# Normalising attention through a transposed, DRAM-spread row of reciprocals, and two early score blocks

## The chip, the cores and the metric

One NeuronCore of a Trainium2 chip runs the whole program. The metric is device time in microseconds of one execution; the kernel before takes 704.56 us as the median of three executions (704.35 to 704.77). TensorE is written PE, VectorE DVE, ScalarE ACT, GpSimd POOL, SyncE (here the main DMA queue) SP.

## The reference, cut to what matters

Attention with pooled queries, then two feed-forward blocks. Batch 2, 8 heads, 1152 keys, 576 pooled queries, head size 64, model width 512.

```python
q_pool = q.reshape(B, H, S // 2, 2, D).mean(axis=3)          # 576 queries
scores = (1.0 / np.sqrt(D)) * np.matmul(q_pool, k^T)
scores = scores - max(scores)
attn = exp(scores);  attn = attn / (sum(attn) + 1e-09)
out = attn @ v                                                # [B, H, 576, 64]
x = out as [1152 tokens, 512];  h = x @ w_in;  x = softplus(h) @ w_out      # d_ff 2048
xn = x / sqrt(mean(x*x) + 1e-06) * rms_g
y = (silu(xn @ w_gate) * (xn @ w_val)) @ w_out2               # d_ff 1536
```

The division by the row sum is what the change is about: every query row of every head has one sum, and the kernel divides after the product with v.

## The kernel before, in words

**Pairs.** The 16 (batch, head) matrices are worked off as eight pairs `pb` of two heads. The 576 queries of a head are four tiles of 128 (`x` = 0 to 3, NF = 4) and a rest of 64; the rests of the two heads share a fifth tile, `x` = NF, the shared tile.

**One tile.** `qk` (line 434) multiplies queries with keys: a query is split in a high and a low part, so that a tile of one head takes 6 matmuls of 384 columns into one of two score areas in PSUM: area A for head 0 and for the shared tile (there 12 matmuls), area B for head 1. `softmax` (457) reduces the negated maximum `nm` on DVE (463) and runs Exp on ACT (465), whose accumulator puts the row sum into a column of `den` (128 x 9: four tiles of each head and the shared one). An area is free again when its Exp has read it. `flip` (473) and `flip_m` (732, for the shared tile) transpose the probabilities on PE, four blocks of 128 x 128 to a PSUM bank, and ACT or DVE copies the bank to `pt`. `av` (492) multiplies `pt` with v into such a bank and copies it to `O`, which holds the output of the pair transposed: head size of both heads along the partitions, 576 queries along the columns.

**Two banks.** All transposes and `av` take their banks in turn from a ring of two (`tbank`, 470): what is to write a bank waits until everything that touched the use two before it is done.

**Normalising.** `scales` (509) adds 1e-9 to `den`, takes reciprocals, and copies each reciprocal 64 times beside itself into `rd` (five blocks of 128 x 128). `spread` (525) transposes those blocks on PE (four blocks in part 0, one in part 1), so that the reciprocals lie along the columns, in the same bank ring, and DVE multiplies `O` with them into `y` (540, 547); then `y` is split in a high and a low part for the next stage.

**Order.** The loop at lines 766 to 799 emits the work; PE's order is the order of emission. `turn` (724) gives the transposes of a tile as a list: T[0], T[1] (4 + 4 of head 0), T[2], T[3] (4 + 4 of head 1), T[4] (the ninth block of both heads); for the shared tile T[0], T[1], T[2] (4, 4, 1). In a tile `x` < 4 the order is T[0], (spread of the pair before, in tiles 1 and 2), scores of `x`+1 into A, T[1], `av` of the tile before, T[2], T[3], scores into B, T[4]. The scores B emitted in tile 3 are those of the next pair's tile 0; its scores A are emitted in the shared tile, after T[0] and T[1].

**The planner.** For the other engines the class `Plan` (63) makes a list schedule out of declared costs: each operation has one or two engines on which it may run, a due time follows from what comes after it, and operations start in order of time. Where ACT and DVE can both do one, SLACK (2.0 us) decides how readily ACT takes it; WAIT (5.0 us) says from which difference in due time an engine is kept for a more urgent operation. DMAs are planned on the SP queue in the same way.

**After attention.** Line 800 on: weights come as 64-bit numbers and are decoded (`decode`, 296) into a high and a low part on ACT, DVE and POOL, 68 pieces in all, 32 of them for the first feed-forward block; slots for 18 pieces open before attention is over, the rest when its buffers are free. Three blocks of 384 tokens go through 16 steps of the first block (a step is 24 matmuls, `terms`, 584) and then 12 of the second.

Of the kernel before, what the change touches and what calls it, by code (L numbers as in the profile page):

```python
# [12 lines left out]
F32 = mybir.dt.float32  # L13
# [3 lines left out]
ALU = mybir.AluOpType  # L17
# [3 lines left out]
P = 128  # L21
B, H, S, D = 2, 8, 1152, 64
SQ = S // 2
# [5 lines left out]
CK = S // P  # L29
NP = B * H // 2  # L30
NF = SQ // P
N = 384
NBLK = NT // N
KB = S // N
# [1 line left out]
MIDDLE = 8  # L36
AFTER = 2 * J1 + 24
SEM = 0.1
SLACK = 2.0
WAIT = 5.0  # L40
WARM = 16
MM = N / 2400 + 0.014

# [19 lines left out]
class Plan:  # L63
# [13 lines left out]
    def op(self, opts, fn, r=(), w=(), lat=0.0, after=()):  # L77
        o = Op()
        o.fn, o.opts, o.lat = fn, opts, lat
        o.deps, o.after, o.succ = set(), set(after), []  # L80
        o.n = len(self.ops)
        for keys, writes in ((r, False), (w, True)):
            for b, part in keys:
                o.deps |= self.before(b, part, writes)
        for keys, writes in ((r, False), (w, True)):
            for b, part in keys:
                (b.writers if writes else b.readers).setdefault(part, []).append(o)
                if not b.ops or b.ops[-1] is not o:
                    b.ops.append(o)
        o.deps.discard(o)  # L90
        self.ops.append(o)
        if opts[0][0] == "PE":
            self.pe.append(o)
        return o
# [101 lines left out]
def dve(n, fast=False, psum=False):  # L196
    t = 0.157 + n / (1920 if fast else 960)
    return ("DVE", t) if psum else ("DVE", t, 1)


def act(n, sbuf=True):
    return "ACT", n / 1400 + (0.28 if sbuf else 0.2)


def pool(n):
    return "POOL", 0.05 + n * 0.00275
# [3 lines left out]
def body(ctx: ExitStack, tc: tile.TileContext, kT, qT, v, w1, w1o, wg, wv, w2o, rg, outT):  # L210
    nc = tc.nc
# [3 lines left out]
    plan = Plan()  # L215
    op = plan.op

    const = ctx.enter_context(tc.tile_pool(name="const", bufs=1))
    ident = const.tile([P, P], F32, name="ident")
    make_identity(nc, ident)  # L220
    ones = const.tile([P, 1], F32, name="ones")
# [26 lines left out]
    def ring(which, tag, shape, dtype=F32, bufs=1):  # L248
        b = plan.ring(tag, bufs, sb(which, tag, shape, dtype, bufs))
        owned[which].append(b)  # L250
        return b

    def copy(e, out, in_):
        if e == "ACT":
            nc.scalar.copy(out, in_)  # L255
        else:
            engines[e].tensor_copy(out, in_)  # L257

    def tt(e, out, in0, in1, o):
        engines[e].tensor_tensor(out=out, in0=in0, in1=in1, op=o)  # L260
# [35 lines left out]
    def decode(n):  # L296
# [26 lines left out]
        if b in third:  # L323
# [4 lines left out]

    qx = [[[fixed("ea"[z], f"q{s}{'AB'[h]}{z}", [P, NF * P + P], F32R) for s in "hl"] for h in range(2)]
          for z in range(2)]  # L330
# [4 lines left out]
    for z in range(2):  # L335
        for h in range(2):
            for s in range(2):
                c = NF * P + (D if h == 0 else 0)
                op([dve(D)], lambda e, b=qx[z][h][s], c=c: copy(e, b()[:, c:c + D], zero), w=[(qx[z][h][s], "z")])

    st = [dict() for _ in range(NP)]

    def prep(pb):
# [7 lines left out]
        kcuts = [(c, slice(c * N, c * N + N), N) for c in range(KB)]  # L351
        f = NF * P
        qcuts = ((0, slice(0, P), P), (1, slice(P, SQ), SQ - P))
# [78 lines left out]
    units = {}  # L432

    def qk(pb, x, h):
# [4 lines left out]
        sc = units[pb, x, h]["s"]  # L439
        heads = (h,) if x < NF else (0, 1)  # L440
        todo = [(hh, z) for hh in heads for z in range(2)]
# [50 lines left out]
    def av(pb, x):  # L492
        s = st[pb]
        pt = units[pb, x, 0]["pt"]
        t = tbank()
        n = P if x < NF else D

        def go(e):
            for c in range(CK):
                for h in range(2):  # L500
                    rhs = pt()[:, c, h, :] if x < NF else pt()[:, c, 0, h * D:h * D + D]
                    nc.tensor.matmul(t()[h * D:h * D + D, :n], lhsT=s["v"][h]()[:, c, :], rhs=rhs,  # L502
                                     start=(c == 0), stop=(c == CK - 1))
        op([("PE", 0.1 + CK * 0.24 * n / P)], go, r=[(pt, None), (s["v"][0], None), (s["v"][1], None)],
           w=[(t, None)])
        o = s["O"]
        op([dve(n, psum=True), act(n, False)], lambda e: copy(e, o()[:, x * P:x * P + n], t()[:, :n]), r=[(t, None)], w=[(o, x)])

    def scales(pb):
        s = st[pb]  # L510
        den = s["den"]
        behind = [units[pb + 1, 0, h]["mx"] for h in range(2) if (pb + 1, 0, h) in units]
        rd = s["rd"] = ring("a", "rdb", [P, NF + 1, 2, D])
        o = op([("DVE", 0.17, 1)], lambda e: nc.vector.tensor_scalar(out=den(), in0=den(), scalar1=1e-9, scalar2=None,
                                                                    op0=ALU.add), w=[(den, None)])
        o.deps.update(behind)
        op([("DVE", 0.25, 1)], lambda e: nc.vector.reciprocal(den(), den()), w=[(den, None)])
        op([dve(NF * P), act(NF * P)], lambda e: copy(
            e, rd()[:, :NF], den()[:, :2 * NF].rearrange("p (h x) -> p x h", h=2).unsqueeze(3).to_broadcast([P, NF, 2, D])),
           r=[(den, None)], w=[(rd, 0)])  # L520
        op([dve(P), act(P)], lambda e: copy(
            e, rd()[:, NF], den()[:, 2 * NF:].unsqueeze(2).to_broadcast([P, 2, D])),
           r=[(den, None)], w=[(rd, 1)])

    def spread(pb, part):
        s = st[pb]
        rd, o = s["rd"], s["O"]
        bank = tbank()
        if part == 0:
            s["y"] = ring("a", "y", [P, SQ])  # L530
        y = s["y"]
        f = NF * P
        xs = range(NF) if part == 0 else (NF,)

        def go(e):
            for i, x in enumerate(xs):
                nc.tensor.transpose(bank()[:, i * P:(i + 1) * P], rd()[:, x].rearrange("p h d -> p (h d)"), ident)  # L537
        op([("PE", 0.09 * len(xs) + 0.03)], go, r=[(rd, part)], w=[(bank, None)])
        if part == 0:
            op([dve(f, psum=True)], lambda e: nc.vector.tensor_tensor(out=y()[:, :f], in0=o()[:, :f], in1=bank()[:, :f], op=ALU.mult),  # L540
               r=[(bank, None), (o, None)], w=[(y, 0)])
            return

        def rest(e):
            for h in range(2):
                p = slice(h * D, h * D + D)
                nc.vector.tensor_tensor(out=y()[p, f:], in0=o()[p, f:], in1=bank()[p, h * D:h * D + D], op=ALU.mult)
        op([("DVE", 0.46)], rest, r=[(bank, None), (o, None)], w=[(y, 1)])
        b, k = divmod(pb, H // 2)
        cuts = ((0, 0, N), (1, 0, SQ - N)) if b == 0 else ((1, SQ - N, N), (2, 0, N))  # L550
        q0 = 0
        for t, a, z in cuts:
            m = z - a
            i = slice(q0, q0 + m)
            o2 = slice(a, z)
            xh, xl = X[t]
            op([dve(m, True), act(m)], lambda e, xh=xh, i=i, o2=o2: copy(e, xh()[:, k, o2], y()[:, i]), r=[(y, None)],
               w=[(xh, (k, a))])
            op([pool(m)], lambda e, xh=xh, xl=xl, i=i, o2=o2: tt(e, xl()[:, k, o2], y()[:, i], xh()[:, k, o2],
                                                                        ALU.subtract),  # L560
               r=[(y, None), (xh, (k, a))], w=[(xl, (k, a))])
            q0 += m
# [203 lines left out]
    for pb in range(NP):  # L766
        last = pb == NP - 1
        for x in range(NF + 1):
            if x == 1 and 0 < pb < NP - 1:
                prep(pb + 1)  # L770
            feed(min(EARLY, 2 * pb + 1) if not last else EARLY + MIDDLE)
            T = turn(pb, x)
            if x < NF:
                T[0]()
                if pb and x in (1, 2):
                    spread(pb - 1, x - 1)
                qk(pb, x + 1, 0)
                T[1]()
                if prev:
                    av(*prev)  # L780
                T[2]()
                T[3]()
                if x < NF - 1:
                    qk(pb, x + 1, 1)
                elif not last:
                    qk(pb + 1, 0, 1)
                T[4]()
            else:
                T[0]()
                T[1]()  # L790
                if not last:
                    qk(pb + 1, 0, 0)
                else:
                    make_banks(1, "h")
                    m1_h(0)
                scales(pb)
                T[2]()
                av(*prev)
            prev = (pb, x)
    m1_h(1)  # L800
    av(*prev)
# [9 lines left out]
    for i in range(n1):  # L811
        t, j = divmod(i, J1)
# [13 lines left out]
    for i in range(n2):  # L826
        n, j = divmod(i, J2)
# [65 lines left out]
```

## Time and profile before

| | |
|---|---|
| median of three executions | 704.56 us (704.35 to 704.77) |
| profiled execution: time, span | 703.74 us, 701.9 us |
| PE busy | 98% of the span |
| DVE, ACT, POOL busy | 62%, 48%, 15% |
| granted TensorE clock | full in all 40 slices |
| attention, from the first scores to the last `av` | 8.4 to 273.0 us |

The busy time of PE covers the time from the start of an instruction to its modelled end, and matmuls overlap, so that the mean of a row is longer than the step from one to the next. What an instruction costs on PE is read from starts: from the start of a run of them to the start of what follows.

### The profile page before, as it was taken

To read this page: it belongs to the slowest core of one execution; us is meant where nothing else is said; L and a number is where in the kernel's file an instruction comes from. 1 tells how busy PE (TensorE), PEld (TensorE's weight loads), DVE (VectorE), ACT (ScalarE), POOL (GpSimd) and SP (SyncE) were. 2 spreads that over 40 slices of the span, in tenths; PEclk is the share of its full clock that TensorE was granted. 3 is DMA by queue.
4 is the path that set the end of the run, shared out by engine and by line. 5 is a ranking of instruction groups with operands and counts; after the bars stand their busy time and mean duration, and the time that the engine had idled before them with its cause. 6 is when DMAs were issued, how large, how long until landed. Compare 5 with 4: busy or idle time off the path is not lost.

```text
span 701.9 us, 12446 instructions
## 1 busy us (share of the span) xinstructions
PE 685.1 (98%) x5099; PEld 659.3 (94%) x5099; DVE 436.1 (62%) x764; ACT 335.4 (48%) x625; POOL 106.7 (15%) x112
## 2 busy tenths in 40 slices
PE   5999999999999999999999999999999999999998
PEld 4989898988989899999999999999999999999997
DVE  6878867778777678898425268898776342222222
ACT  3878777877787786554222143455452110010001
POOL 1432524334332023000000000011121000000000
PEclk9999999999999999999999999999999999999999
DMA  7545324241402112454100023353451100010001
GB/s 199 164 122 143 102 66 126 92 146 36 132 7 90 61 62 91 155 176 149 61 1 1 1 87 111 122 159 96 154 173 61 46 1 0 1 46 1 1 0 46
DMA packets 18856, 57.68 MB, mean 82 GB/s; under 512 B 2416, under 2 KB 5360, under 8 KB 18800
## 3 DMA queue, kind: packets, MB, share of 16 engines
q1 hardware_dynamic: 18080, 56.63, 26.1%
q8 instruction: 40, 0.66, 0.4%
q10 hardware_dynamic: 720, 0.26, 0.2%
q14 instruction: 16, 0.13, 0.1%
HBM read 54.53 MB, written 2.36 MB: 81 GB/s over the span
## 4 chain that ended last, share of the span: by engine, by line
PE 94%; DVE 2%; ACT 2%; DMA 1%; issue 1%; SPq 0%; DVEq 0%; ACTq 0%
PE s L585 15%; PE s L587 15%; PE s L586 15%; PE s L447 12%; PE t L484 10%; PE t L502 9%; PE t L587 5%; PE t L586 5%; PE t L585 5%; DVE nm L463 1%; ACT p L465 1%; PE t L741 1%; PE t L537 1%; DMA p<-in_qT_dram 1%; DMA kr<-in_kT_dram 0%
## 5 line engine op out<-in xcount | busy, mean ns | idle before, releaser
L585 PE MATMUL s<-x,w 128*128 128x384 f32 x348 | 117.4, 337 | 0.5 <-ACT rs L255 0.5
L463 DVE TENSOR_REDUCE nm<-s 128x1 f32<-128x1152 f32 x72 | 97.8, 1358 | 31.1 <-PE s L447 24.8
L587 PE MATMUL s<-x,w 128*128 128x384 f32 x348 | 116.7, 335 | 0.0
L586 PE MATMUL s<-x,w 128*128 128x384 f32 x348 | 116.6, 335 | 0.0
L465 ACT ACTIVATE p<-s,nm 128x1152 f32<-128x1152 f32 x72 | 88.0, 1223 | 16.5 <-DVE nm L463 14.4
L255 ACT COPY pt<-t 128x512 f32<-128x512 f32 (+1 forms) x140 | 72.2, 523 | 35.6 <-PE t L484 28.0
L484 PE MATMUL t<-ident,p 128*128 128x128 f32 x576 | 83.3, 279 | 4.8 <-ACT p L465 4.3
L707 ACT ACTIVATE g<-s 128x384 f32<-128x384 f32 x36 | 17.7, 491 | 139.8 <-PE s L587 139.7
L585 PE MATMUL s<-gh,w 128*128 128x384 f32 x243 | 81.5, 335 | 0.0
L587 PE MATMUL s<-gh,w 128*128 128x384 f32 x243 | 81.5, 335 | 0.0
L586 PE MATMUL s<-gl,w 128*128 128x384 f32 x243 | 81.4, 335 | 0.0
L484 PEld LDWEIGHTS t<-ident,p 128*128 128x128 f32 x576 | 65.8, 141 | 15.4 <-ACT p L465 6.2
L502 PE MATMUL t<-pt,v 128*64 128x128 f32 (+1 forms) x1440 | 80.1, 265 | 0.0
L502 PEld LDWEIGHTS t<-pt,v 128*64 128x64 f32 x1440 | 71.3, 137 | 7.3 <-issue 5.8
L585 PEld LDWEIGHTS s<-x,w 128*128 128x128 f32 x348 | 65.4, 188 | 1.0 <-ACT rs L255 0.8
L586 PEld LDWEIGHTS s<-x,w 128*128 128x128 f32 x348 | 65.4, 188 | 0.0
L587 PEld LDWEIGHTS s<-x,w 128*128 128x128 f32 x348 | 65.4, 188 | 0.0
L309 ACT ACTIVATE t<-raw 128x512 f32<-128x512 f32 x68 | 45.1, 670 | 14.4 <-DVE w L260 8.2
L607 ACT ACTIVATE g<-s 128x384 f32<-128x384 f32 x36 | 17.7, 491 | 71.1 <-PE s L587 68.1
L260 DVE TENSOR_TENSOR gl<-g,gh 128x384 fp32r<-128x384 f32 x83 | 46.3, 558 | 7.8 <-ACT gh L255 5.5
L257 DVE CAST gh<-g 128x384 fp32r<-128x384 f32 x62 | 22.5, 364 | 45.7 <-PE t L587 41.0
L319 DVE SCALAR_TENSOR_TENSOR t<-t,t 128x512 int32<-128x512 int32 x68 | 47.6, 700 | 1.6
(134 smaller groups left out, 1208.1 us busy)
## 6 DMA issues: line engine op xcount, KB each, us to landing
raw<-in_w_dram SPq DMA_DIRECT2D x16, 512.0 KB, 3.4
raw<-in_w1o_dram SPq DMA_DIRECT2D x16, 512.0 KB, 3.4
qr<-in_qT_dram SPq DMA_DIRECT2D x28, 288.0 KB, 4.4
raw<-in_wg_dram SPq DMA_DIRECT2D x12, 512.0 KB, 3.5
raw<-in_wv_dram SPq DMA_DIRECT2D x12, 512.0 KB, 3.5
raw<-in_w2o_dram SPq DMA_DIRECT2D x12, 512.0 KB, 3.5
v<-in_v_dram SPq DMA_DIRECT2D x16, 288.0 KB, 3.2
kr<-in_kT_dram SPq DMA_DIRECT2D x7, 576.0 KB, 4.9
```

What stands on the lines that cost most here:

```text
L255: nc.scalar.copy(out, in_)
L260: engines[e].tensor_tensor(out=out, in0=in0, in1=in1, op=o)
L309: o = op([("ACT", 0.68)], lambda e: nc.scalar.activation(out=t0(), in_=word(1).bitcast(F32), scale=2.0 ** -112, **(dict(func=AF.Prelu, alp ...
L319: op([dve(DM)], lambda e: nc.vector.scalar_tensor_tensor(out=t0().bitcast(I32), in0=t0().bitcast(I32), scalar=3, in1=t1(), op0=ALU.logical ...
L447: nc.tensor.matmul(sc()[:, c, :N], lhsT=q, rhs=s["kk"][hh]()[:, c * N:(c + 1) * N], start=(hh == heads[0] and z == 0), stop=(hh == heads[- ...
L463: u["mx"] = op([dve(S, psum=True)], lambda e: nc.vector.tensor_reduce(out=nm(), in_=sc()[:, :, :N], axis=AX.XY, op=ALU.max, negate=True), ...
L465: o = op([("ACT", 1.42)], lambda e: nc.scalar.activation(out=pr(), in_=sc()[:, :, :N], func=AF.Exp, bias=nm(), accum_out=s["den"]()[:, col ...
L484: nc.tensor.transpose(t()[:, i * P:(i + 1) * P], pr[:, c * P:(c + 1) * P], ident)
L502: nc.tensor.matmul(t()[h * D:h * D + D, :n], lhsT=s["v"][h]()[:, c, :], rhs=rhs, start=(c == 0), stop=(c == CK - 1))
L585: nc.tensor.matmul(out, lhsT=w[:, 0, cols], rhs=hi, start=start, stop=False)
L586: nc.tensor.matmul(out, lhsT=w[:, 0, cols], rhs=lo, start=False, stop=False)
L587: nc.tensor.matmul(out, lhsT=w[:, 1, cols], rhs=hi, start=False, stop=stop)
```

## The change

The row sums of the seven pairs that have a pair behind them go another way. The `av` of the shared tile transposes `den` (128 x 9) into the free columns of its own bank, so that 9 rows of 128 sums come out; DVE adds 1e-9, takes reciprocals, and one DMA writes them to a DRAM scratch (9 runs of 512 bytes); four DMAs read them back into `rd`, spread over the 64 partitions of each head. One multiplication over 576 columns, on DVE or POOL, gives `y` (`shift`). The `spread` calls of these pairs go. In the shared tile both score blocks of the next pair are emitted there: A ahead of T[0], B after T[1]; tile 3 emits none for the next pair. SLACK becomes 1.0 and WAIT 2.0. The last pair keeps the old way.

```diff
-SLACK = 2.0
-WAIT = 5.0
+SLACK = 1.0
+WAIT = 2.0
+    rows = [dram.tile([C, P], F32, name=f"row{pb}", tag=f"row{pb}") for pb in range(NP - 1)]      # C = 9
...  av
+        spill = x == NF and pb < NP - 1
+            if spill:
+                nc.tensor.transpose(t()[:C, P:2 * P], s["den"](), ident)
...  scales, for pb < NP - 1
+        sums = ring("a", "sums", [C, P])
+        op([("DVE", 0.3)], lambda e: nc.vector.tensor_scalar(out=sums(), in0=bank()[:C, P:2 * P], scalar1=1e-9, scalar2=None,
+                                                            op0=ALU.add), r=[(bank, None)], w=[(sums, None)])
+        op([("DVE", 0.45, 1)], lambda e: nc.vector.reciprocal(sums(), sums()), w=[(sums, None)])
+        op([("SP", 0.9)], lambda e: nc.sync.dma_start(out=rows[pb], in_=sums()), r=[(sums, None)], w=[(row, None)], lat=4.0)
+        for h in range(2):
+            for to, c, n in ((0, h * NF * P, NF * P), (NF * P, 2 * NF * P + h * D, D)):
+                op([("SP", 0.6)], lambda e, h=h, to=to, c=c, n=n: nc.sync.dma_start(
+                    out=rd()[h * D:h * D + D, to:to + n], in_=flat()[c:c + n].unsqueeze(0).to_broadcast([D, n])),
+                   r=[(row, None)], w=[(rd, (h, to))], lat=6.0)
+    def shift(pb):
+        y = s["y"] = ring("a", "y", [P, SQ])
+        op([dve(SQ), pool(SQ)], lambda e: tt(e, y(), s["O"](), s["rd"]()[:, :SQ], ALU.mult),
+           r=[(s["O"], None), (s["rd"], None)], w=[(y, None)])
+        split(pb)
...  the loop, x < NF
                 T[0]()
-                if pb and x in (1, 2):
-                    spread(pb - 1, x - 1)
                 qk(pb, x + 1, 0)
                 T[1]()
                 if prev:
                     av(*prev)
+                if pb and x == 0:
+                    scales(pb - 1)
+                    shift(pb - 1)
                 T[2]()
                 T[3]()
                 if x < NF - 1:
                     qk(pb, x + 1, 1)
-                elif not last:
-                    qk(pb + 1, 0, 1)
                 T[4]()
...  the loop, x == NF
+                if not last:
+                    qk(pb + 1, 0, 0)
                 T[0]()
                 T[1]()
                 if not last:
-                    qk(pb + 1, 0, 0)
+                    qk(pb + 1, 0, 1)
-                scales(pb)
                 T[2]()
                 av(*prev)
+                if last:
+                    scales(pb)
```

## Rows read from the trace of the kernel before

**Rows 1.** Page, busy us of each engine (share of the span), instructions:
```profile
PE 685.1 (98%) x5099; PEld 659.3 (94%) x5099; DVE 436.1 (62%) x764; ACT 335.4 (48%) x625; POOL 106.7 (15%) x112
```
**Rows 2.** Waits of PE, 20 to 280 us: total us, times, longest
```profile
PE t L484 <- ACT p L465: 4.1, 7, 0.6
```
**Rows 3.** Waits of PE, 280 to 702 us
```profile
PE s L585 <- ACT rs L255: 0.5, 1, 0.5
```
**Rows 4.** PE in order of time, one change of pair: start, length, [idle before]
```profile
97.90 0.82 PE L484 MATMUL t<-ident,p 128*128 128x128 f32 x6
98.48 0.77 PE L447 MATMUL s<-kk,qhA 128*128 128x384 f32 x3
...
103.29 1.12 PE L484 MATMUL t<-ident,p 128*128 128x128 f32 x8
104.17 0.77 PE L447 MATMUL s<-kk,qhB 128*128 128x384 f32 x3
...
105.51 1.28 PE L741 MATMUL t<-ident,p 128*128 128x128 f32 x8
106.55 0.77 PE L447 MATMUL s<-kk,qhA 128*128 128x384 f32 x3
...
107.88 2.19 PE L502 MATMUL t<-pt,v 128*64 128x128 f32 x36
110.64 0.66 PE L484 MATMUL t<-ident,p 128*128 128x128 f32 x4 [0.57 <-ACT p L465]
...
113.91 1.09 PE L484 MATMUL t<-ident,p 128*128 128x128 f32 x8
...
115.90 0.84 PE L484 MATMUL t<-ident,p 128*128 128x128 f32 x6
116.74 0.66 PE L537 MATMUL t<-ident,rdb 128*128 128x128 f32 x4
117.15 0.78 PE L447 MATMUL s<-kk,qhA 128*128 128x384 f32 x3
...
122.94 0.82 PE L484 MATMUL t<-ident,p 128*128 128x128 f32 x6
...
123.87 0.77 PE L447 MATMUL s<-kk,qhA 128*128 128x384 f32 x3
```
**Rows 5.** DVE in the same stretch
```profile
107.88 1.36 DVE L463 TENSOR_REDUCE nm<-s 128x1 f32<-128x1152 f32 x1 [0.37 <-PE s L447]
...
114.05 0.23 DVE L257 COPY O<-t 128x64 f32<-128x64 f32 x1 [0.31 <-PE t L502]
```
**Rows 6.** PE late in the last pair
```profile
262.28 1.12 PE L484 MATMUL t<-ident,p 128*128 128x128 f32 x8
263.61 0.44 PE L484 MATMUL t<-ident,p 128*128 128x128 f32 x2 [0.21 <-ACT pt L255]
```
**Rows 7.** Groups by line, whole span: busy us, mean ns, idle before
```profile
L465 ACT ACTIVATE p<-s,nm 128x1152 f32<-128x1152 f32 x72 | 88.0, 1223 | 16.5 <-DVE nm L463 14.4
L257 DVE COPY O<-t 128x128 f32<-128x128 f32 (+1 forms) x35 | 9.7, 276 | 15.3 <-PE t L502 15.2
```
**Rows 8.** Waits of the SP queue: total us, times, longest
```profile
SPq L264 <- DVE t L314: 194.8, 58, 9.5
```
**Rows 9.** DMA issues: KB each, median us to landing
```profile
v<-in_v_dram SPq DMA_DIRECT2D x16, 288.0 KB, 3.2
...
out_dram<-t SPq DMA_DIRECT2D x6, 192.0 KB, 1.9
```
**Rows 10.** A stretch: us, busy PE, PEld, DVE, ACT, POOL, clock, DMA, GB/s
```profile
300.00:320.00 20.00, 20.00 (x117) 20.00 (x116) 17.49 (x32) 10.80 (x21) 0.00 (x0) 1.00 0.50 163
```
**Rows 11.** DVE at a weight decode, 327 us
```profile
327.26 0.69 DVE L260 TENSOR_TENSOR w<-t,w 128x512 fp32r<-128x512 f32 x1
```
**Rows 12.** PE at the 14th step of the first feed-forward block
```profile
327.79 0.34 PE L585 MATMUL t<-x,w 128*128 128x384 f32 x1
...
328.14 0.34 PE L587 MATMUL t<-x,w 128*128 128x384 f32 x1
```

More of the change, by code (lines that the diff above doesn't have):

```diff
@@ L31 @@
 NF = SQ // P
+C = 2 * NF + 1
 N = 384
@@ L218, in body @@
     const = ctx.enter_context(tc.tile_pool(name="const", bufs=1))
+    dram = ctx.enter_context(tc.tile_pool(name="dram", bufs=1, space=bass.MemoryType.DRAM))
+    rows = [dram.tile([C, P], F32, name=f"row{pb}", tag=f"row{pb}") for pb in range(NP - 1)]
     ident = const.tile([P, P], F32, name="ident")
@@ L496, in av @@
         n = P if x < NF else D
+        spill = x == NF and pb < NP - 1
+        if spill:
+            s["bank"] = t
         def go(e):
@@ L503, in go @@
                                      start=(c == 0), stop=(c == CK - 1))
-        op([("PE", 0.1 + CK * 0.24 * n / P)], go, r=[(pt, None), (s["v"][0], None), (s["v"][1], None)],
-           w=[(t, None)])
+            if spill:
+                nc.tensor.transpose(t()[:C, P:2 * P], s["den"](), ident)
+        op([("PE", 0.1 + CK * 0.24 * n / P + 0.12 * spill)], go,
+           r=[(pt, None), (s["v"][0], None), (s["v"][1], None)] + [(s["den"], None)] * spill, w=[(t, None)])
         o = s["O"]
@@ L511, in scales @@
         den = s["den"]
-        behind = [units[pb + 1, 0, h]["mx"] for h in range(2) if (pb + 1, 0, h) in units]
-        rd = s["rd"] = ring("a", "rdb", [P, NF + 1, 2, D])
-        o = op([("DVE", 0.17, 1)], lambda e: nc.vector.tensor_scalar(out=den(), in0=den(), scalar1=1e-9, scalar2=None,
+        rd = s["rd"] = ring("a", "rdb", [P, (NF + 1) * P])
+        if pb == NP - 1:
+            op([("DVE", 0.17, 1)], lambda e: nc.vector.tensor_scalar(out=den(), in0=den(), scalar1=1e-9, scalar2=None,
@@ L515, in scales @@
                                                                     op0=ALU.add), w=[(den, None)])
[L516 to L523, printed above, removed]
+            op([("DVE", 0.25, 1)], lambda e: nc.vector.reciprocal(den(), den()), w=[(den, None)])
@@ new lines, in scales @@
+            wide = lambda: rd().rearrange("p (x h d) -> p x h d", h=2, d=D)
+            op([dve(NF * P), act(NF * P)], lambda e: copy(
+                e, wide()[:, :NF], den()[:, :2 * NF].rearrange("p (h x) -> p x h", h=2).unsqueeze(3).to_broadcast([P, NF, 2, D])),
+               r=[(den, None)], w=[(rd, 0)])
+            op([dve(P), act(P)], lambda e: copy(
+                e, wide()[:, NF], den()[:, 2 * NF:].unsqueeze(2).to_broadcast([P, 2, D])),
+               r=[(den, None)], w=[(rd, 1)])
@@ new lines, in scales @@
+            return
+        bank = s["bank"]
+        sums = ring("a", "sums", [C, P])
+        op([("DVE", 0.3)], lambda e: nc.vector.tensor_scalar(out=sums(), in0=bank()[:C, P:2 * P], scalar1=1e-9, scalar2=None,
+                                                            op0=ALU.add), r=[(bank, None)], w=[(sums, None)])
+        op([("DVE", 0.45, 1)], lambda e: nc.vector.reciprocal(sums(), sums()), w=[(sums, None)])
+        row = plan.buf(lambda: rows[pb])
+        op([("SP", 0.9)], lambda e: nc.sync.dma_start(out=rows[pb], in_=sums()), r=[(sums, None)], w=[(row, None)], lat=4.0)
@@ new lines, in scales @@
+        flat = lambda: rows[pb].rearrange("c q -> (c q)")
+        for h in range(2):
[4 more added lines that the diff above has]
+    def shift(pb):
+        s = st[pb]
+        y = s["y"] = ring("a", "y", [P, SQ])
+        op([dve(SQ), pool(SQ)], lambda e: tt(e, y(), s["O"](), s["rd"]()[:, :SQ], ALU.mult),
+           r=[(s["O"], None), (s["rd"], None)], w=[(y, None)])
+        split(pb)
@@ L536, in go @@
             for i, x in enumerate(xs):
-                nc.tensor.transpose(bank()[:, i * P:(i + 1) * P], rd()[:, x].rearrange("p h d -> p (h d)"), ident)
+                nc.tensor.transpose(bank()[:, i * P:(i + 1) * P], rd()[:, x * P:(x + 1) * P], ident)
         op([("PE", 0.09 * len(xs) + 0.03)], go, r=[(rd, part)], w=[(bank, None)])
@@ L548, in spread, with split @@
         op([("DVE", 0.46)], rest, r=[(bank, None), (o, None)], w=[(y, 1)])
+        split(pb)
+    def split(pb):
+        y = st[pb]["y"]
         b, k = divmod(pb, H // 2)
```

## The prediction

> **What bounds the kernel now.** The first view is the page's list of engines: PE is busy for 98% of the span and the next engine, DVE, for 62% [rows 1]. So the next question is not which engine is full but where PE still waits, and the waits of PE answer it by stage. In the attention stage there is one regular wait: seven times, 4.1 us in all, the transposes of a tile wait for the Exp of its scores [rows 2]. Seven is the number of changes from one pair to the next. After attention PE waits for 0.5 us in all [rows 3]. So a change is worth what it takes out of PE's own list of instructions, plus what it takes out of these seven waits, less the waits that it adds; work on DVE, ACT and POOL counts only through PE's waits.
>
> The third view is PE in order of time over one change of pair [rows 4]. The reader is to see two things in it: what the blocks of the spread cost PE between the blocks around them, and why the wait at 110.64 us is there. The scores A of the next pair start at 106.55, the last `av` of the old pair ends at 107.88 + 2.19 = 110.07, and the first transposes of the next pair come 0.57 us after that, because their Exp is not done: after the scores come one maximum of 1.36 us [rows 5] and one Exp of 1.22 us [rows 7].
>
> **The change part by part**, per change of pair, of which there are seven.
>
> 1. *Spread transposes go.* With no spread, six probability transposes take 98.48 - 97.90 = 0.58 us up to the scores that follow. With part 0 in between it is 117.15 - 115.90 = 1.25, with part 1 it is 123.87 - 122.94 = 0.93 [rows 4]. The spread costs 0.67 + 0.35 = 1.02 us, the wait for the third bank in a row included. Minus 1.02.
>
> The Trainium skill ("TensorE: Matmul & The Clock Gate", Part 4: PE-mode transpose) gives a transpose of 128 x 128 in a kernel as about 275 ns. The trace agrees as to the length of one record, but not as to its price: eight start and make way for the scores in 104.17 - 103.29 = 0.88 us [rows 4]. By that figure of the Trainium skill the five would be worth an estimated 1.38 us, seven pairs 2.5 us more than I count, and the forecast would stand at 695.8, inside its own range below; I take the starts.
>
> 2. *The wait for the Exp goes.* In the new order the scores A come behind T[4] of tile 3. Between their end and the end of that `av` PE then has eight transposes (0.88), scores B and one transpose (107.88 - 106.55 = 1.33) and the `av` (2.19), 4.4 us in all [rows 4]. Maximum and Exp need 1.36 + 1.22 = 2.58 [rows 5, 7]. The 1.8 us left over cover a DVE or ACT instruction that stands ahead. Scores B are needed only by T[2], later still. Area A itself is free in time: its Exp for the shared tile has `av` and ten transposes to run beside. What would be late next is scores A, if that Exp slipped by over 1 us. Minus 4.1/7 = 0.59.
>
> 3. *T[4] becomes the third bank in a row.* Today scores B stand between T[3] and T[4]; tomorrow nothing does. The last pair already has that order: T[4] starts 263.61 - 262.28 = 1.33 us after the eight in front of it, not 0.88 [rows 6]. Plus 0.45. In return the eight transposes of the shared tile, today behind T[4], get scores in front: they take 106.55 - 105.51 = 1.04 today and should take 0.88. Minus 0.16.
>
> 4. *One transpose more*, of `den`. Nearest rows: 0.88/8 = 0.11 in a run, 0.35 for the single one of the spread, with its wait. It stands on its own behind the `av` but shares its bank, so it waits for none: plus 0.11, bounds 0 and 0.35.
>
> 5. *The bank of that `av` is held longer.* T[3] of the next tile needs it. Today the copy to `O` starts 0.14 us after the `av` (114.05 against 113.91) and takes 0.23 [rows 4, 5]. Then the addition of 1e-9 has to read 128 columns; the nearest row is the copy of `O`, 0.276 [rows 7]. That ends near 114.55, with a handover 114.6; T[3] would want to start at 113.91 + 0.44 = 114.35. Plus 0.25. Bounds: 0 if ACT takes the copy and DVE adds first, and 0.25 + 1.36 if a maximum stands between on DVE.
>
> 6. *DVE, ACT.* Gone from them: two small operations on `den`, two copies into `rd`, three multiplications. New: the addition, a reciprocal over 128 columns, one multiplication over 576 columns. None is on PE's path but the addition; cost nothing while the cover of point 2 holds. The reciprocal has no near row (`den` has 9 columns); even at 1 us it stands behind the addition and in front of maxima that have over 1.8 us of cover.
>
> 7. *The DMAs.* One write and four reads on SP per pair, the reads queued behind the wait for the write. The nearest rows land in 1.9 us (out) and 3.2 us (in) [rows 9], so `rd` is there some 6 us after the reciprocals with the issues, at worst twice that. By the costs declared in the change the planner expects 0.9 + 4.0 + 0.6 + 6.0 = 11.5 us, and nobody but the multiplication waits for it; `y` is due a pair later. Loads of the next pair stand behind the wait on SP for some 2 us and are used a pair later. Nothing.
>
> 8. *SLACK and WAIT* change choices on ACT and DVE everywhere. They can win little, since PE waits for only 0.5 us in the feed-forward blocks [rows 3]; they can lose where a maximum or a weight gets late. Bounds: 1 us gained, 5 us lost (one DVE instruction of 0.69 us [rows 11] too much in PE's way at each of seven changes); I take nothing.
>
> 9. *The first feed-forward block.* From the release of the buffers for 8 weight slots, at the end of pair 6, to the end of attention the stretch gets 1.02 us shorter, for the spread of pair 6 lies in it. The decode fed from there has no room: the low part of a weight is made at 327.26 + 0.69 [rows 11], and PE, whose step starts at 327.79, reads it with its third matmul at 328.14 [rows 12]; DVE is busy for 87% there [rows 10]. DVE loses some work in that stretch too, so I take half: plus 0.5, bounds 0 and 1.5.
>
> Sum: 7 x (-1.02 - 0.59 + 0.45 - 0.16 + 0.11 + 0.25) = 7 x (-0.96) = -6.7, and with 0.5 back, -6.2 us. The profiled execution took 703.74 us, 1.84 beside its span; 703.74 - 6.2 = 697.5. The median of the runs is 0.8 above that execution, so the forecast is **698.3 us**.
>
> **The rivals.**
>
> *A. The banks cost nothing.* If copies are placed so that T[4] and T[3] don't wait (points 3 and 5 at -0.16 in sum) and the decode keeps up, it is 7 x (-1.02 - 0.59 - 0.16 + 0.11) = -11.6: 692.9. Against it: the wait of point 3 stands in a row.
>
> *B. The decode or the bank takes half.* A maximum between `av` and the addition at half of the changes costs 3.5 x 1.36 = 4.8 us: 703.1. For it: at 107.88 and after each block of scores DVE is in a maximum of 1.36 us [rows 5]; against it: behind the shared `av` DVE sat idle for 0.31 us [rows 5].
>
> *C. No difference.* The decode decides the first block: with the high parts of nine pieces moved from ACT to DVE by the smaller SLACK, at 0.69 us each [rows 11], 6.2 us would be put back: 704.5. For it: DVE at 87% against ACT at 54% [rows 10].
>
> *D. Slower: the multiplication stalls DVE.* SP works in order, and a weight load waits there 194.8/58 = 3.4 us on average and up to 9.5 for its buffer [rows 8]. If such a load stands ahead of the write, `rd` comes 6 + 9.5 = 15.5 us after the reciprocals, 4.0 later than planned; DVE stands at the multiplication, and what goes beyond the 1.8 us of point 2 PE waits: 2.2 us, and then for the work piled up on DVE, some 2 us for a maximum and a copy. At seven changes 7 x 4.2 = 29 us less 6.2: up to 727; at three of them 711. It turns slower from a mean delay of 0.9 us of PE per change. Against it: the planner may give the multiplication to POOL, and knows the queue.
>
> **How the numbers follow.** Forecast, with its own range of 695.5 to 701.5: 0.50. A, down to 692: 0.17. B: 0.14. C: 0.07. D: 0.12, with any other stall that the new order brings. What this measurement can tell from no change is about 0.2%, 1.4 us. Faster: 0.50 + 0.17 + 0.14 = 0.81; the same 0.07; slower 0.12. The range from 692.5 to 704.8 leaves out most of D and the far end of A.
>
> **What would show it.** In the waits of PE: the seven on the Exp gone, in their place waits of T[4] (0.2 to 0.5 us) and T[3] on copies or on the addition. In PE's order: no L537 but for five at the end, and the way from pair to pair 0.96 us shorter. In the waits of PE after attention: the wait for a weight near the 14th step. A wait of DVE on the DMA of `rd` would show D. The prediction is wrong if PE waits for scores A because area A isn't free, if transposes gone from PE don't bring the starts together, or if the feed-forward stage gets longer by more than 1.5 us.

## The result and the profile after

The changed kernel takes 697.28 us (median of four, 696.19 to 697.86) against 704.45 of the kernel before: a ratio of 0.9899, 95% interval 0.9887 to 0.991, so 7.2 us faster where 6.2 were forecast. Its profiled execution took 697.78 us, 6.0 less than the one of before; the rows below are from that one, so they can account for 6.0 us. The rest of the 7.2 is scatter between executions: the profiled one of before lay 0.7 us below the median of its kernel, this one 0.5 above.

The engines, to be held against [rows 1]: PE has 3.9 us less to do and stays at 98%.

```profile
PE 681.2 (98%) x5071; PEld 657.5 (95%) x5071; DVE 430.7 (62%) x741; ACT 335.2 (48%) x617; POOL 111.9 (16%) x115
```

The waits of PE in attention (total us, times, longest), to be held against [rows 2]: the seven waits for the Exp are gone, and the waits for banks that the forecast named have come. The first row holds six waits of T[4] at changes, that of the last pair, and one of 0.7 us that is taken up at the end; the third is the seventh of T[4]; the second and fourth are the seven of T[3].

```profile
PE t L487 <- ACT pt L258: 2.2, 8, 0.7
PE t L487 <- DVE sums L535: 0.8, 5, 0.2
PE t L487 <- DVE pt L260: 0.3, 1, 0.3
PE t L487 <- DVE O L260: 0.3, 2, 0.2
```

PE in order of time over one change of pair, to be held against [rows 4].

```profile
101.24 1.12 PE L487 MATMUL t<-ident,p 128*128 128x128 f32 x8
102.57 0.44 PE L487 MATMUL t<-ident,p 128*128 128x128 f32 x2 [0.21 <-ACT pt L258]
102.77 0.77 PE L450 MATMUL s<-kk,qhA 128*128 128x384 f32 x3
...
103.90 1.04 PE L774 MATMUL t<-ident,p 128*128 128x128 f32 x8
104.69 0.77 PE L450 MATMUL s<-kk,qhB 128*128 128x384 f32 x3
...
106.02 2.19 PE L508 MATMUL t<-pt,v 128*64 128x128 f32 x36
108.14 0.66 PE L487 MATMUL t<-ident,p 128*128 128x128 f32 x4
...
110.21 1.27 PE L508 MATMUL t<-pt,v 128*64 128x64 f32 x36
111.41 0.28 PE L511 MATMUL t<-ident,den 128*9 128x128 f32 x1
111.52 0.60 PE L487 MATMUL t<-ident,p 128*128 128x128 f32 x4
112.28 0.63 PE L487 MATMUL t<-ident,p 128*128 128x128 f32 x4 [0.16 <-DVE O L260]
...
113.79 0.82 PE L487 MATMUL t<-ident,p 128*128 128x128 f32 x6
114.36 0.77 PE L450 MATMUL s<-kk,qhA 128*128 128x384 f32 x3
```

The reader is to see the two waits in brackets, of T[4] and of T[3]; the first transposes of the next pair at 108.14, straight behind the `av` (before, 0.57 us later); and six transposes that make way for the scores in 0.57 us, with no spread between.

From one shared `av` to the next it was 31.77 us (112.71 to 144.48) before and is now 30.64 (110.21 to 140.85). Over all seven the mean falls from (271.83 - 48.77)/7 = 31.87 to (265.37 - 48.73)/7 = 30.95. The first feed-forward matmul starts 6.46 us sooner, and the stage behind it takes 437.0 us instead of 436.9. All of the gain lies in attention, and at most 0.1 us of it is given back. Before, then after:

```profile
265.03 0.42 PE L585 MATMUL s<-x,w 128*128 128x384 f32 x1
```
```profile
258.57 0.42 PE L618 MATMUL s<-x,w 128*128 128x384 f32 x1
```

### The profile page after: what moved, and what is told of

Same layout as the page of the kernel before. It is cut to its first block, busy times and chain, and to the rows that moved or that the text cites. A ratio compares the mean times of both kernels' runs of the same rounds, so it can differ in the third digit from the quotient of the medians.

```text
span 695.6 us, 12413 instructions
## 1 busy us (share of the span) xinstructions
PE 681.2 (98%) x5071; PEld 657.5 (95%) x5071; DVE 430.7 (62%) x741; ACT 335.2 (48%) x617; POOL 111.9 (16%) x115
## 4 chain that ended last, share of the span: by engine, by line
PE 70%; ACT 0%; DVE 0%; issue 0%
PE s L618 15%; PE s L620 15%; PE s L619 15%; PE t L620 5%; PE t L618 5%; PE t L619 5%; PE t L508 3%; PE s L450 3%; PE t L487 2%; PE t L774 0%; PE s L688 0%; ACT pt L258 0%; PE s L716 0%; PE t L566 0%; DVE raw L260 0%
## 5 line engine op out<-in xcount | busy, mean ns | idle before, releaser
L258 ACT COPY pt<-t 128x512 f32<-128x512 f32 (+1 forms) x146 | 76.0, 528 | 36.4 <-PE t L487 29.8
L487 PE MATMUL t<-ident,p 128*128 128x128 f32 x576 | 85.7, 281 | 3.6 <-ACT pt L258 2.2
L263 DVE TENSOR_TENSOR gl<-g,gh 128x384 fp32r<-128x384 f32 x84 | 48.7, 580 | 11.5 <-ACT gh L258 9.3
```

What stands on the lines that cost most here:

```text
L487: nc.tensor.transpose(t()[:, i * P:(i + 1) * P], pr[:, c * P:(c + 1) * P], ident)
```

## The experiments

My theory: the gain is PE's own list (the spread) plus the wait for the Exp, less two new waits for banks. The rivals: the two planner constants made it; the decode gives a part back; the DMA round trip is what could have lost it. Each kernel ran on one chip together with the kernel before (704.45 to 704.62 us there). The third column is the mean of the seven ways from one shared `av` to the next in the profiled execution.

| kernel | median us | way | largest wait of PE in attention |
|---|---|---|---|
| before | 704.5 | 31.87 | Exp, 4.1 us |
| after | 697.28 | 30.95 | copies, 2.2 |
| after, old constants | 697.28 | 30.83 | copies, 1.3 |
| before, new order only | 701.75 | 31.47 | copies, 1.5 |
| after, old order (spread and new constants) | 700.87 | 31.31 | Exp, 4.1 |
| before, new constants only | 703.89 | 31.82 | Exp, 4.0 |
| T[4] later | 697.77 | 30.77 | copies ahead of `av`, 2.4 |
| sums in the single flip | 696.80 | 30.52 | copies, 1.7 |
| both | 693.22 | 30.11 | 1.3 |
| both, old constants | 698.21 | 30.96 | copies ahead of `av`, 4.6 |
| after, latencies 0 | 704.54 | 32.06 | `O`, 6.4 |
| after, fewer slots | 698.49 | 30.97 | copies, 2.5 |

**The three parts.** First the constants put back:

```diff
-SLACK = 1.0
-WAIT = 2.0
+SLACK = 2.0
+WAIT = 5.0
```

> The changed kernel with SLACK and WAIT put back to 2.0 and 5.0. My theory: the gain comes from PE's own list and the seven waits for the Exp, not from the two constants, so this takes 697.3 us give or take 1. Rival: the constants place the copies so that PE does not wait; then without them the waits of PE in attention (3.6 us in all in the changed kernel) grow and it takes 700 us or more.

697.28 us (0.9892, 0.9879 to 0.9906): the same median. Then the order alone, in the kernel before:

```diff
-                elif not last:
-                    qk(pb + 1, 0, 1)            # tile 3
...
+                if not last:
+                    qk(pb + 1, 0, 0)            # shared tile, ahead of T[0]
                 T[0]()
                 T[1]()
                 if not last:
-                    qk(pb + 1, 0, 0)
+                    qk(pb + 1, 0, 1)
```

> The kernel before with only the order changed: both score blocks of the next pair in the shared tile, reciprocals still spread by five transposes on PE, old constants. My theory: the seven waits for the Exp go (0.59 each) and the eight transposes no longer wait (0.16), T[4] waits 0.45: 7 x -0.30 = -2.1 us, 702.4. Rival: the order brings nothing by itself, because the spread transposes then wait longer for their banks: 704 us or more.

701.75 us (0.9956, 0.9944 to 0.9969), minus 2.8 where 2.1 were expected. The seven Exp waits are replaced by seven of T[4], one at each change:

```profile
PE t L484 <- ACT pt L255: 1.5, 7, 0.2
```

The spread without the order is the changed kernel with that edit taken back; it keeps the new constants:

> The changed kernel with the old order of the score blocks: spread through DRAM, new constants. My theory: -1.02 for the spread, +0.11 for the transpose of the sums, +0.25 for the bank: 7 x -0.66 = -4.6 us, 699.9. Rival: the wait for the Exp, still there, grows by the DVE work that the normalising now puts behind it, and half of this is lost: 702 us.

700.87 us (0.9943, 0.9931 to 0.9956), minus 3.7 where 4.6 were expected; the Exp waits are there as before, 4.1 us, and did not grow, so the rival falls on that, though its time is not far off.

```profile
PE t L487 <- ACT p L468: 4.1, 7, 0.6
```

And the constants alone, in the kernel before (the first diff the other way round):

> The kernel before with only SLACK 1.0 and WAIT 2.0. My theory: no difference, 704.5 us give or take 0.7, since PE waits for nothing that another placing could take away but the seven Exp waits, which lie between PE, DVE and ACT in a fixed order. Rival: the constants are a part of the gain, 703 us or less.

703.89 us (0.999, 0.9981 to 0.9999): at most a small gain, 0.65 us. The run of the spread holds the new constants already, so the parts to add are its 3.7 us (interval 3.1 to 4.9) and the 2.8 of the order (2.2 to 3.9): 6.5 us, together 7.2. Within the intervals the two parts add; they stand at different places of PE's list.

**The latencies declared to the planner.**

```diff
...  the write
-        ... w=[(row, None)], lat=4.0)
+        ... w=[(row, None)], lat=0.0)
...  the reads
-        ... w=[(rd, (h, to))], lat=6.0)
+        ... w=[(rd, (h, to))], lat=0.0)
```

> The changed kernel with the two latencies that the planner is told of the DRAM round trip set to zero, so that the multiplication is planned about 3 us after the reciprocals, long before the data is there. If the DMA chain is some 6 us and only the declared latency hides it (my rival D of a stalled multiplication), DVE or POOL waits some 3 us at each of seven pairs, and where it is DVE the time grows by 1 to 3 us each: 700 to 712 us. If DVE has enough room, it stays at 697.3.

704.54 us (0.9998, 0.998 to 1.0016; single executions took from 701.58 to 706.80): the whole gain is lost. At all seven pairs the multiplication now waits for its data, five times on POOL and twice on DVE, and PE waits for a copy of DVE:

```profile
POOL y L263 <- DMA rdb<-row: 24.6, 5, 13.3
DVE y L263 <- DMA rdb<-row: 6.5, 2, 4.4
PE t L487 <- DVE O L260: 6.4, 5, 3.6
```

What this costs PE is uneven. Where DVE stands, PE stands behind it: 1.25 us at one pair, 3.56 at another, here the multiplication and then PE:

```profile
190.19 0.76 DVE L263 TENSOR_TENSOR y<-O,rdb 128x576 f32<-128x576 f32 x1 [4.39 <-DMA rdb<-row]
```
```profile
192.81 0.65 PE L487 MATMUL t<-ident,p 128*128 128x128 f32 x4 [3.56 <-DVE O L260]
```

After those 3.56 us of idle PE the granted clock averages 0.60 from 193 to 197 us, for part of that time at the lower level of 1.2 GHz, which costs an estimated 4 x 0.40 = 1.6 us more (three matmuls of 384 columns take 1.16 us at 193.86, 0.68 elsewhere); this way takes 36.11 us. At two pairs where POOL multiplies, PE loses 0.73 and 0.72 us behind a DVE instruction that runs beside that multiplication and is stretched (1.78 us where 0.69 is usual; see the last section). Two ways are undisturbed (30.73 and 30.79). The edit changes only what the planner is told; the multiplication moves forward in the queues, and other operations move with it. Rival D's mechanism is real, and in the changed kernel, where the latencies are declared, no multiplication is listed as waiting for its data.

**Fewer weight slots.**

```diff
-MIDDLE = 8
+MIDDLE = 5
```

> The changed kernel with MIDDLE 5 instead of 8: three weight slots fewer are open before the end of attention, so three decodes move behind it. My step 9 said that the decode has no room in the first feed-forward block. If that is so, PE waits there for about 3 pieces x 2.3 us of DVE work each, some 7 us, and the time is 703 to 705 us. Rival: the low part of 0.2 us before its use was chance, the planner simply made it late because it could; then PE waits for less than 2 us, and it takes 697 to 699 us.

698.49 us (0.9914, 0.9901 to 0.9928), within the rival's range. In the waits of PE behind attention not one is for a weight; the only one is the 0.5 us of [rows 3]. But the edit did not do what was expected of it. Before the first feed-forward matmul the traces of both kernels show twelve low parts decoded, and at the step that [rows 12] shows the low part is made at the same time as in the changed kernel (318.63):

```profile
318.65 0.69 DVE L263 TENSOR_TENSOR w<-t,w 128x512 fp32r<-128x512 f32 x1
```

No decode moved behind attention, so this run does not test step 9; what does is the changed kernel itself, under point 9 below. Where the 1.2 us come from is open; the profiled execution shows 0.4 of them behind attention.

**The two new waits.** T[4] behind scores A, and the single transpose of the shared tile ahead of T[1]:

```diff
...  tile 3
-                T[4]()
+                if x < NF - 1 or last:
+                    T[4]()
...  the shared tile, not last
                 qk(pb + 1, 0, 0)
+                turn(pb, NF - 1)[4]()
                 T[0]()
-                T[1]()
                 qk(pb + 1, 0, 1)
                 T[2]()
+                T[1]()
```

> The changed kernel with T[4] of tile 3 behind scores A instead of ahead of them, and the single transpose of the shared tile ahead of T[1]: no three banks in a row. My theory: T[4] waits 0.45 us for its bank seven times in the changed kernel; here it does not, and the last av waits at most 0.1 for the bank of the single transpose: 7 x -0.35 = -2.5 us, 694.8. Rival: the wait only moves, scores A come 0.65 us sooner and wait for area A, and the time stays at 697.3.

697.77 us (0.9903, 0.9886 to 0.9919): no gain in time. Undisturbed ways do get shorter, by 0.2 to 0.3 us of the 0.35 expected (30.33 to 30.44 us), but three times the `av` of tile 3 now waits up to 0.9 us, not 0.1, for the bank of the single transpose, whose copy ACT does late:

```profile
PE t L508 <- ACT pt L258: 2.4, 3, 0.9
```

Then the sums transposed in the bank of the shared tile's single transpose, in the order of the changed kernel (the same lines go from `av`, and `scales` of the pair is called ahead of the last `av` of the shared tile):

```diff
 def flip_m(pb, c0, n):
+        spill = c0 == 8 and pb < NP - 1
...
+            if spill:
+                nc.tensor.transpose(t()[:C, P:2 * P], den(), ident)
```

> The changed kernel with the transpose of the sums in the bank of the shared tile's single transpose, which is not used again before the av has run, instead of the bank of the shared av. My theory: T[3] then waits for the copy of O alone; the 0.3 us that it waits today for copy and addition go: 7 x -0.3 = -2.1 us, 695.2. Rival: DVE is late anyway and the wait stays or goes to T[0]: 697 us.

696.80 us (0.989, 0.9875 to 0.9905), minus 0.5 where 2.1 were expected. Attention gains more than that: the waits of T[3] are gone, only those of T[4] are left, the ways are 30.48 us nearly throughout and the last shared `av` starts 3.1 us sooner than in the changed kernel. The feed-forward stage takes 438.6 us instead of 437.0: three steps at its start come late, two of them with these rows. Why DVE is late there was not tried; at 264.25 and 269.84 us two of its decode instructions take 1.5 us instead of 0.69, beside POOL (see the last section).

```profile
268.75 0.41 PE L612 MATMUL t<-x,w 128*128 128x384 f32 x1 [0.32 <-DVE y L570]
279.89 0.44 PE L613 MATMUL s<-gl,w 128*128 128x384 f32 x1 [0.33 <-DVE gl L263]
```

Both together: the order of the run with T[4] behind scores A, and the sums in T[4]'s bank (columns 2P to 3P) instead of that of the `av`; only the lines that are not in the diffs above:

```diff
 def flip(pb, x, todo):
+        spill = n == 2 and x == NF - 1 and pb < NP - 1
...
+            if spill:
+                nc.tensor.transpose(t()[:C, 2 * P:3 * P], den(), ident)
...
                 qk(pb + 1, 0, 0)
+                turn(pb, NF - 1)[4]()
+                scales(pb)
```

> Both: T[4] behind scores A, and the sums transposed in T[4]'s bank. My theory: the gains add, 7 x -0.65 = -4.5 us: 692.7. Rival: with the waits for banks gone another bound comes up, DVE or ACT, at 82% of a pair that is now shorter, and it takes 695 us or more.

693.22 us (0.9841, 0.9827 to 0.9856): 11.2 us under the kernel before and 4.1 under the changed one, near the 4.5 expected, in part by luck. Six of the seven ways take 30.0 us, and all seven gain 7 x 0.84 = 5.9 us in the profiled execution; but the first shared `av` starts at 51.00 instead of 48.73, since the first scores come 1.1 us later and two `av` of the first pair wait 1.3 us for copies. PE in order of time, at the same place as above:

```profile
102.29 1.12 PE L491 MATMUL t<-ident,p 128*128 128x128 f32 x8
103.17 0.77 PE L450 MATMUL s<-kk,qhA 128*128 128x384 f32 x3
...
104.29 0.38 PE L491 MATMUL t<-ident,p 128*128 128x128 f32 x2
104.51 0.27 PE L493 MATMUL t<-ident,den 128*9 128x128 f32 x1
104.62 0.60 PE L779 MATMUL t<-ident,p 128*128 128x128 f32 x4
104.98 0.78 PE L450 MATMUL s<-kk,qhB 128*128 128x384 f32 x3
...
112.16 1.09 PE L491 MATMUL t<-ident,p 128*128 128x128 f32 x8
113.01 0.77 PE L450 MATMUL s<-kk,qhB 128*128 128x384 f32 x3
```

No bracket is left here: T[2] and T[3] make way after 0.88 us in tile 3 and after 0.85 in the next pair's tile 0, and T[4], the sums and T[0] stand between the score blocks. The same with the old constants:

> The version with T[4] behind scores A and the sums in T[4]'s bank, with SLACK 2.0 and WAIT 5.0 as in the kernel before. My theory: its two waits of an av for a copy in the first pair (1.3 us) come from where the planner puts copies, so the constants can move them: 692 to 694 us, no more than 1 us from 693.2. Rival: with the banks free, the constants matter, and it is over 695 us.

698.21 us (0.9913, 0.9899 to 0.9926), 5.0 more: my theory was wrong here. One row tells it; at each of the seven changes the `av` waits some 0.66 us for the bank of the single transpose. DVE copied it at once in the run before (at 106.42 us, 0.29); here the planner leaves the copy to ACT, which is in an Exp until 106.3.

```profile
PE t L515 <- ACT pt L258: 4.6, 7, 0.7
```

So the constants decide nothing in the changed kernel and 5 us in this one: in this order the bank of the single transpose is wanted again 0.66 us after it (106.11 and 106.77 us in the run before).

## Why the prediction was right, and where not

By its own points, per change of pair:

1. *Spread*, minus 1.02: the rows with L537 are gone from seven pairs, and the six transposes in front of scores take 0.57. Shown, with the run of the spread without the order.
2. *Exp*, minus 0.59: gone in the changed kernel and in the order-only run, there in the run of the spread. From start to start it gave more than its idle time, 0.64: the first transposes came 110.64 - 107.88 = 2.76 us after the start of the `av`, now 108.14 - 106.02 = 2.12.
3. *T[4]*, plus 0.45: 102.57 - 101.24 = 1.33, the figure of [rows 6] to the hundredth. The eight transposes of the shared tile: 104.69 - 103.90 = 0.79, so they gave 0.25 back, not 0.16.
4. *The transpose of the sums*, plus 0.11: 111.52 - 111.41 = 0.11.
5. *The bank of the shared `av`*, plus 0.25: T[3] starts 112.28 - 111.52 = 0.76 after T[2] instead of 0.44, so 0.32. DVE adds first and copies `O` then, 0.28 and 0.20 us:

```profile
111.72 0.28 DVE L535 TENSOR_SCALAR sums<-t 9x128 f32<-9x128 f32 x1 [0.43 <-PE t L511]
111.93 0.20 DVE L260 COPY O<-t 128x64 f32<-128x64 f32 x1
...
112.77 0.93 DVE L537 RECIPROCAL sums<-sums 9x128 f32<-9x128 f32 x1
```

6. *DVE*: the reciprocal takes 0.93 us, at the end of what I allowed, and nobody waits for it.
7. *The DMAs* hide, on SP in this order:

```profile
113.72 0.29 SPq L539 DMA_DIRECT2D row<-sums  x1
114.12 0.34 SPq L267 DMA_DIRECT2D kr<-in_kT_dram  x1
115.25 2.38 SPq L543 DMA_DIRECT2D rdb<-row  x4
```

The fourth read is issued near 117.0, and a read lands 3.4 us after its issue at the median (2.8 to 5.0), so the data is there between 120 and 121, some 7 us after the reciprocals end at 113.70. I had said 6, the planner counts on 11.5; the multiplication of this pair starts at 127.97.

8. *SLACK and WAIT*, nothing: so it was for this change. That they had no part in a shorter order was not said, and would have been wrong.
9. *The decode*, plus 0.5: this is the term that failed. It measured 0.1, and PE never waited for a weight. At the same step, and at the same place in the order of the decodes, the low part is now made at 318.63 + 0.69 and read at 321.68:

```profile
318.63 0.69 DVE L263 TENSOR_TENSOR w<-t,w 128x512 fp32r<-128x512 f32 x1
```
```profile
321.68 0.34 PE L620 MATMUL t<-x,w 128*128 128x384 f32 x1
```

That is 2.4 us of room instead of 0.2, though the step itself comes 6.46 us sooner. In the run with both edits the feed-forward stage starts 10.1 us sooner than before (at 254.97) and takes 437.3 us, again without a wait for a weight. So step 9 read a coincidence as a limit: a planner that works by due times may make a thing late because it can, and being just in time is by itself no sign of a bound.

With the rows of after the sum per change is -1.02 - 0.64 + 0.45 - 0.25 + 0.11 + 0.32 = -1.03; the way shown above got shorter by 1.13, and 0.10 is not placed. Against it stands one change that took 31.66 us (171.72 to 203.38): PE waits there 0.69 us for a copy, the longest of all its waits. So the forecast was right in its mechanism, point by point, and its total came out so near partly by luck: the 0.5 us that it gave to the decode did not come, and 0.9 us was lost at this one change, for which it had no term. Rival A needed the two bank waits gone, and only the run with both edits shows that it could be had, by another order and not by another placing of copies; B, C and D did not come.

## What to carry to other kernels

Where one engine does all the work in a fixed order, price an edit by the starts around a block, not by the lengths of its records, and look in the trace for a place that already has the new order: [rows 6] gave the new wait exactly. Where transposes pass through a ring of two banks, a third bank in a row cost 0.45 us here and another reader on a bank that is soon used again 0.3 us; look for a bank with time to spare, and see who makes its copy. The detour through DRAM cost PE nothing where the planner was told how long it takes, and the whole gain where it was not.

## What the runs showed of the hardware

**DVE beside POOL.** The change that took 31.66 us begins with two DVE instructions with SBUF inputs that are stretched while POOL works:

```profile
180.95 1.22 DVE L322 SCALAR_TENSOR_TENSOR t<-t,t 128x512 int32<-128x512 int32 x1
182.10 1.54 DVE L263 TENSOR_TENSOR qs<-qr 128x288 f32<-128x288 f32 x1
```
```profile
180.81 0.81 POOL L263 TENSOR_TENSOR qs<-qr 128x288 f32<-128x288 f32 x1 [6.39 <-DMA qr<-in_qT_dram]
182.00 1.32 POOL L263 TENSOR_TENSOR w<-t,w 128x512 fp32r<-128x512 f32 x1 [0.37 <-ACT w L258]
```

The first kind takes 0.69 us at the median, and at most that in all 65 of the 68 places where no POOL instruction runs beside it; the second takes 0.43 to 0.46 us in three of its four other places. Not every one beside POOL is stretched, and the maxima, which read PSUM, take 1.36 us with POOL and without. The maxima behind the two start late, the Exp after them, and then the copy for which PE waits:

```profile
184.94 1.22 ACT L468 ACTIVATE p<-s,nm 128x1152 f32<-128x1152 f32 x1 [1.78 <-DVE nm L466]
```
```profile
186.78 1.36 PE L487 MATMUL t<-ident,p 128*128 128x128 f32 x8 [0.69 <-ACT pt L258]
```

The run with fewer slots, planned alike at this place, shows it again (1.30 and 1.55 us, then a wait of 0.79). The Trainium skill ("GPSIMD Engine Reference", 1. Specifications) says that SBUF interfaces are shared with VectorE, with contention for instructions with two SBUF inputs; the trace agrees. That these POOL instructions cost PE its 0.69 us was not tried by moving them.

**The clock at the start.** In some executions of several of these kernels the view of stretches lists a lower granted clock of TensorE in the first 20 us. In the run with the sums in the single flip the stretch from 10 to 15 us is at 0.50, which is the level of 1.2 GHz; in the profiled execution of the changed kernel it is listed at 1.00.

```profile
10.00:15.00 5.00, 3.09 (x8) 2.18 (x8) 4.48 (x9) 1.31 (x3) 0.00 (x0) 0.50 0.83 231
```
```profile
10.00:15.00 5.00, 3.51 (x10) 2.77 (x10) 4.55 (x9) 2.04 (x4) 0.00 (x0) 1.00 0.80 206
```

PE's own rows don't bear that difference out. Three matmuls of 384 columns take 1.16 us in both stretches, first in the run with the flip, then in the changed kernel, and 0.68 us in the changed kernel from 21 us on:

```profile
11.82 1.16 PE L450 MATMUL s<-kk,qlA 128*128 128x384 f32 x3
```
```profile
10.90 1.16 PE L450 MATMUL s<-kk,qlA 128*128 128x384 f32 x3
...
21.05 0.68 PE L450 MATMUL s<-kk,qlB 128*128 128x384 f32 x3
```

So both executions ran this stretch equally slowly, and the 1.00 listed for it (with it the "full in all 40 slices" of the kernel before, which has 1.16 us there too, at 11.64) can't be taken for the speed of the matmuls. Nothing in the comparison hangs on it: the first shared `av` starts at 48.66 us where 0.50 is listed and at 48.73 where 1.00 is.
